# Attention scores of two heads at once in 64-row tiles, with the heads packed by pair, in an attention and MoE kernel on one core

## The chip, the core and the metric

The kernel runs on one core of one Trainium2 chip. The metric is the device time of one execution in microseconds (us), as the median of several runs. The profile is one further execution, taken by the hardware profiler.

## What is computed

Attention over 2 batches of 8 heads, with queries averaged by twos, then a dense mixture of four experts, then an ELU network. All is float32. Cut to what matters here:

```python
def _attn_ref(q, k, v):                      # (2, 8, 1152, 64) each
    q_pool = q.reshape(B, H, S // 2, 2, D).mean(axis=3)
    scores = np.matmul(q_pool, k.transpose(0, 1, 3, 2)) / np.sqrt(D)
    scores = scores - np.max(scores, axis=-1, keepdims=True)
    attn = np.exp(scores)
    attn = attn / (np.sum(attn, axis=-1, keepdims=True) + 1e-09)
    return np.matmul(attn, v)
...
x = attn_out.transpose(0, 2, 1, 3).reshape(B * S // 2, H * D)   # (1152, 512)
x = _moe_ref(x=x, domain_probs, w1, w2)      # sum over e of p_e * relu(x @ w1[e]) @ w2[e]
return _moe2_ref(x=x, w_in, w_out)           # ELU(x @ w_in) @ w_out
```

A head has 576 pooled queries, 1152 keys and a head dimension of 64.

## The kernel before, in words

The program has two stages. The first is the attention of 16 heads, two heads to a pair. The second, some two thirds of the time, is the MoE and the ELU network (called the MoE here): long runs of matmuls of 288 and 384 columns (line 1092) by a variant of Strassen's method, for which each quarter of the activations is split into a high and a low part and the two are multiplied crosswise.

Precise products are made in the same way in the attention. Queries and keys are split into a high part (rounded to the fast matmul type f32r) and a low part (the remainder). In `scores` (line 820) the contraction has 128 rows: `ks` holds the high part of a head's keys in rows 0 to 63 and the low part in rows 64 to 127, and `qs` holds the queries' high part in both halves, and then the low part in both halves. Two matmuls then give all four products of one head. The 1152 queries of a pair are cut into nine blocks of 128 rows (`m` from 0 to 8); block 4 holds the last 64 rows of one head and the first 64 of the other and takes four matmuls in place of two. A block's 1152 keys are taken in a part of 512 columns (`z` = 0) and one of twice 320 (`z` = 1), each with two PSUM buffers of its own.

Each block then runs through these steps, named by the letter that the planner uses:

- R (`max_all`, VectorE) takes the row maxima, E (`exp`, ScalarE, line 837) writes the exponentials to one of five tiles `e`.
- T (`transposes`, line 882) transposes 128x128 pieces, three to a PSUM bank `t`, of which there are two; D and G (`evac`, line 608 in a helper) copy them to the tile `pt` of the whole head, on ScalarE or VectorE.
- V (`values`, line 905) multiplies with the values when a whole head is transposed. An output has 64 rows (the head dimension), so two query halves of 288 columns go to the two halves of the array's columns: a form of the array of 128 rows by 64 columns. These are plain f32, and the program's one matmul is two instructions in the trace. O copies the result to `xo`.
- I, U, J, K, M, N form the softmax factors of a head. The step 3 writes them to DRAM (`dr`), the step 4 loads them back spread over the partitions (`fb`), X (`x_scaled`) multiplies, and the step m copies the head by DMA to its place in `acc`, the activations. The last two heads' X runs on VectorE.
- q, k, A, B, C, r, F, W, s load a pair's queries and keys, split them, and copy the two parts by DMA to the halves of `qs` and `ks`.

The order of all this on each engine is not written by hand: `order_of` plays the steps through with the costs in `STAGES` and ranks with the offsets in `MORE`, and the instructions are emitted in that order. The MoE has a planner of its own (`ffn_order`). Near the end of the attention, steps h and i already split two of the four quarters of `acc` for the MoE: x12 and x22 (quarters 8 and 3). x11 (heads 8 to 11 of the 16) and x21 (heads 12 to 15) are split in the MoE. Its first eight units use x12 and x22, the next four x11, and four more x21, whose parts go to a tile named `K`. Four PSUM banks `p` hold the running sums; each comes free when the hidden values in it were scaled (line 1151), rounded to `hh` and subtracted to `hl`.

Of the kernel before, what the change touches and what calls it, by code (L numbers as in the profile page):

```python
# [14 lines left out]
ALU = mybir.AluOpType  # L15
# [12 lines left out]
    "S": (dict(PE=465), 8),  # L28
    "R": (dict(DVE=690), 8),
    "E": (dict(ACT=790), 4),  # L30
    "I": (dict(DVE=220), 1.2),
    "U": (dict(POOL=400), 1.2),
    "J": (dict(ACT=250), 1.5),
    "K": (dict(POOL=600), 1.2),
    "M": (dict(DVE=200), 1.2),
    "N": (dict(POOL=400), 1.2),
    "3": (dict(SP=500), 2),
    "4": (dict(SP=1700), 2),
    "X": (dict(POOL=2300), 6),
    "T": (dict(PE=327), 2),  # L40
    "D": (dict(ACT=480, DVE=557), -3),
    "G": (dict(ACT=480, DVE=557), -4),
    "V": (dict(PE=2140), 6),
    "O": (dict(ACT=400, DVE=460), 0),
    "H": (dict(ACT=440), 8),
    "L": (dict(POOL=810), 3),
# [5 lines left out]
    "q": (dict(SP=450), -9),  # L52
    "k": (dict(SP=450), -9),
    "A": (dict(POOL=1430), -4),
    "B": (dict(ACT=690), -4),
    "C": (dict(DVE=800), -3),
    "r": (dict(SP=2400), -3),
    "F": (dict(ACT=690, DVE=470), -4),
    "W": (dict(POOL=1430), -3),
    "s": (dict(SP=2800), -3),  # L60
    "m": (dict(SP=2300), 8),
# [3 lines left out]
    "y": (dict(SP=600), 20),  # L65
# [3 lines left out]
    "i": (dict(POOL=2700, DVE=1250), 30),  # L69
# [4 lines left out]
AFTER = 240000  # L74

LAG = {"PE": 190, "ACT": 210, "DVE": 220, "POOL": 210, "SP": 9500}
LATE = {"3": 12000, "4": 11500, "r": 8000, "s": 8000, "X": 1200, "U": 900, "K": 700}

MIXED = {"D": dict(ACT=320, DVE=330), "G": dict(ACT=320, DVE=330)}
SECOND = {"S": dict(PE=585), "R": dict(DVE=822), "E": dict(ACT=920), "V": dict(PE=2620)}  # L80

LAST = {"X": dict(DVE=1100)}
MB = 9
NP = 5
CUT = 4

FIRST = [(x, i, z) for i in (0, 1) for x, z in (("q", 0), ("k", 0), ("k", 1), ("q", 1))]
FIRST = {x: 3800 + 1000 * n for n, x in enumerate(FIRST)}

BANKS = {"S0": 2, "S1": 2, "T": 2}  # L90
VBANK = "S0", "S0"

MORE = {
# [20 lines left out]
def blocks_of(i):  # L114

    return range(MB * (i // 2) + 4 * (i % 2), MB * (i // 2) + 5 + 4 * (i % 2))


def names_of(x, *k):

    k = list(k)
    p, m = divmod(k.pop(0), MB) if x in "SRETDG" and k else (0, 0)
# [3 lines left out]
    elif x in "qkABCrFWs":  # L126
        p, m, k = k[0], 0, k[1:]
# [5 lines left out]
def attention_ops(NH, KC):  # L133
# [87 lines left out]
    return ops  # L221


def order_of(ops):

# [1032 lines left out]
```

## Time and profile before

| | |
|---|---|
| median of 3 runs | 835.06 us (834.77 to 839.13) |
| profiled execution | 835.81 us, span 834.0 us |
| TensorE busy | 819.6 us, 98% of the span |
| VectorE, ScalarE, GpSimd busy | 589.3, 428.1, 322.4 us |
| attention, by the trace | first scores at 6.14 us, first matmul of the MoE at 248.25 us |

The span reaches from the first to the last instruction; what is left to the execution's own time lies around it. A matmul's duration in the trace reaches from its start to its modelled end, and successive matmuls overlap, so what one adds to a run of them is read from the distance of their starts or from a run's length, not from its duration.

### The profile page before, as it was taken

The numbers are of one execution on the slowest core, as the hardware profiler recorded it, in microseconds if no ns is written. First come the engines' busy times: TensorE is split into PE (matmuls) and PEld (weight loads), VectorE is DVE, ScalarE is ACT, GpSimd is POOL, SyncE is SP. The second block draws the span as 40 slices with busy tenths as digits, with TensorE's granted clock in tenths as the row PEclk, the third lists the DMA queues.
The fourth block names the chain that finished last, engine by engine and source line by source line (L and its number), as shares of the span: only waits on it lengthen the run. The fifth ranks groups of instructions, "written<-read, shape, count | busy, mean of one in ns | idle before, by whom it ended". The sixth has DMA issues, their size and how long they took to land.

```text
span 834.0 us, 14379 instructions
## 1 busy us (share of the span) xinstructions
PE 819.6 (98%) x5518; PEld 762.5 (91%) x5518; DVE 589.3 (71%) x922; ACT 428.1 (51%) x883; POOL 322.4 (39%) x344
## 2 busy tenths in 40 slices
PE   8999999999997999999999999999999999999998
PEld 7778777777767999999999999999999999999998
DVE  8777777767655849577685848577689857877472
ACT  6787677777763345141424324142434927455370
POOL 4353434344235726363644536263631231313000
PEclk9999999999999999999999999999999999999999
DMA  7999877864215224241422224241431324121002
GB/s 262 184 211 167 198 175 187 186 159 95 65 26 180 89 75 158 69 157 39 153 85 99 86 77 139 75 170 39 140 122 58 111 71 145 39 89 64 1 19 96
DMA packets 48356, 95.02 MB, mean 114 GB/s; under 512 B 14368, under 2 KB 26144, under 8 KB 45344
## 3 DMA queue, kind: packets, MB, share of 16 engines
q1 hardware_dynamic: 48000, 92.47, 39.8%
q10 hardware_dynamic: 288, 1.64, 0.7%
q8 instruction: 43, 0.70, 0.4%
q14 instruction: 25, 0.20, 0.1%
HBM read 64.37 MB, written 10.84 MB: 90 GB/s over the span
## 4 chain that ended last, share of the span: by engine, by line
PE 92%; DVE 3%; DMA 2%; ACT 2%; issue 0%; POOL 0%; SPq 0%; DVEq 0%
PE p L1092 66%; PE s L820 9%; PE s L905 8%; PE t L882 8%; DMA fb<-dr 1%; ACT e L837 1%; DMA q<-in 1%; ACT pt L608 1%; DVE hl L611 0%; DMA dr<-st 0%; DVE p L1151 0%; DVE st L831 0%; DVE K L611 0%; POOL st L611 0%; DVE acc L611 0%
## 5 line engine op out<-in xcount | busy, mean ns | idle before, releaser
L1092 PE MATMUL p<-hl,w2h 128*128 128x384 f32 x576 | 192.6, 334 | 0.5 <-DVE hl L611 0.5
L1092 PE MATMUL p<-hh,w2l 128*128 128x384 f32 x576 | 192.5, 334 | 0.0
L1092 PE MATMUL p<-hh,w2h 128*128 128x384 f32 x576 | 192.4, 334 | 0.0
L611 DVE TENSOR_TENSOR acc<-p,acc 128x768 f32<-128x768 f32 (+1 forms) x61 | 57.5, 942 | 89.5 <-PE p L1092 89.4
L831 DVE TENSOR_REDUCE st<-s 128x1 f32<-128x512 f32 (+1 forms) x144 | 105.4, 751 | 17.5 <-PE s L820 13.9
L1063 POOL TENSOR_TENSOR nt<-nt,ne 128x512 f32<-128x512 f32 x32 | 42.7, 1336 | 193.0 <-DVE ne L1059 193.0
L820 PE MATMUL s<-K,Q 128*128 128x320 f32 (+1 forms) x480 | 109.2, 355 | 0.7 <-ACT e L837 0.7
L837 ACT ACTIVATE e<-s,st 128x512 f32<-128x512 f32 (+1 forms) x144 | 106.5, 747 | 6.2 <-DVE st L831 3.3
L1092 PEld LDWEIGHTS p<-hl,w2h 128*128 128x128 f32 x576 | 108.1, 188 | 0.9 <-DVE hl L611 0.9
L1092 PEld LDWEIGHTS p<-hh,w2l 128*128 128x128 f32 x576 | 108.1, 188 | 0.0
L1092 PEld LDWEIGHTS p<-hh,w2h 128*128 128x128 f32 x576 | 108.1, 188 | 0.0
L882 PEld LDWEIGHTS t<-ident,e 128*128 128x128 f32 x648 | 75.3, 140 | 23.2 <-issue 7.4
L882 PE MATMUL t<-ident,e 128*128 128x128 f32 x648 | 93.7, 276 | 2.7 <-ACT e L837 2.0
L1092 PE MATMUL p<-K,wh 128*128 128x288 f32 x448 | 90.7, 296 | 0.0
L608 ACT CAST hh<-p 128x576 fp32r<-128x576 f32 x78 | 50.0, 641 | 69.8 <-DVE p L1151 66.9
L820 PEld LDWEIGHTS s<-K,Q 128*128 128x128 f32 x480 | 73.8, 189 | 7.3 <-issue 1.8
L905 PE MATMUL s<-pt,v 128*64 128x288 f32 x576 | 76.7, 411 | 0.0
L608 ACT COPY pt<-t 128x384 f32<-128x384 f32 (+1 forms) x126 | 55.3, 456 | 36.3 <-PE t L882 31.9
L1092 PEld LDWEIGHTS p<-K,wh 128*128 128x128 f32 x448 | 72.3, 189 | 0.3 <-DVE p L611 0.2
L1092 PE MATMUL p<-XH,wh 128*128 128x288 f32 x224 | 66.8, 298 | 5.6 <-DVE hl L611 5.1
L608 DVE COPY pt<-t 128x384 f32<-128x384 f32 (+1 forms) x114 | 56.0, 503 | 20.7 <-PE t L882 17.8
L1092 PE MATMUL p<-XH,wl 128*128 128x288 f32 x224 | 66.4, 296 | 0.0
(108 smaller groups left out, 1657.6 us busy)
## 6 DMA issues: line engine op xcount, KB each, us to landing
d<-in_va SPq DMA_DIRECT2D x16, 512.0 KB, 4.0
w<-nt SPq DMA_DIRECT2D x32, 256.0 KB, 3.4
d<-in_vb SPq DMA_DIRECT2D x16, 512.0 KB, 4.1
w<-w SPq DMA_DIRECT2D x8, 1024.0 KB, 4.8
Q<-q SPq DMA_DIRECT2D x28, 288.0 KB, 7.0
w<-in_wa SPq DMA_DIRECT2D x7, 1024.0 KB, 7.0
w<-in_wb SPq DMA_DIRECT2D x7, 1024.0 KB, 4.8
v<-in_v SPq DMA_DIRECT2D x16, 288.0 KB, 6.8
```

The costliest lines, as they stand in the source:

```text
L608: (nc.scalar.copy if e == "ACT" else engines[e].tensor_copy)(out, a)
L611: engines[e].tensor_tensor(out=out, in0=a, in1=b, op=op)
L820: nc.tensor.matmul(out=t[:, j], lhsT=q[:, o : o + P], rhs=ks[p % 2][:, y, c : c + PARTS[z][1]], start=k == x == 0, stop=2 * k + x == last,)
L831: nc.vector.tensor_reduce(out=nm[b, z], in_=s_t[b, z], axis=AX.XY, op=ALU.max, negate=True)
L837: nc.scalar.activation(et[b % NP][:, part(z)].rearrange("p (j k) -> p j k", j=PARTS[z][0]), s_t.pop((b, z)), AF.Exp, bias=nm.pop((b, z)), ...
L882: nc.tensor.transpose(t[:, c * P : c * P + P], et[b % NP][:, (3 * u + c) * P : (3 * u + c + 1) * P], ident)
L905: nc.tensor.matmul(out=tb[i, h][64 * z : 64 * z + 64, :HQ], lhsT=raws[i, "v"][:, c, :], rhs=pt[i % 2][:, c, half(z)], start=c == cs[0], st ...
L1063: nc.gpsimd.tensor_tensor(out=nt, in0=nt, in1=ne, op=ALU.add)
L1092: nc.tensor.matmul(out=out, lhsT=w[a][:, c, m * P : m * P + P], rhs=x[b][:, c], start=new and c == a + b == 0, stop=c == cs - 1 and a == 1 ...
```

## The change

It concerns the attention alone, and the splits that hand over to the MoE.

- The unit of work is no longer a block of one head but 128 queries of both heads of a pair (four units), and a tail unit with the last 64 queries of both. Rows 0 to 63 of `qs` and `ks` hold the pair's first head, rows 64 to 127 its second.
- `scores` makes three products of 64 rows for each head (high by high, high by low, low by high; low by low is dropped), the two heads in turn, into different PSUM banks: a form of the array of 64 rows by 128 columns, two tiles. In the tail unit, the queries of each head stand in their own rows and in 64 of the 128 columns, with zeros elsewhere, and three products of 128 rows do for both. A score step takes both PSUM buffers of its `z`.
- The parts are computed in place, by one operation for the two heads; the copies of queries and keys by DMA (r, s) are gone.
- Transposes stand four to a bank, and a fifth bank holds the last piece of both heads. Six tiles `e`, five tiles `pt` of one unit each.
- `values` works by unit: 128 columns (64 in the tail unit), the two heads in the two halves of the array's columns.
- The factors, their DMAs and X work by pair; X writes to `acc` itself, and the copy m is gone.
- x11 (quarter 1) is split in the attention too; the tiles of quarters 6 and 7 change place.
- Costs, ranks and a table of engines (`ON`) set a new order.

```diff
-        def scores(e, b, z, n):
-            p, m = divmod(b, MB)
-            s_t[b, z] = t = s_bank[z][n][:, :, : PARTS[z][1]]
-
-            hs = [0] * (m <= MH) + [1] * (m >= MH)
-            last = 2 * len(hs) - 1
-            q = qs[p % 2].rearrange("p y x q -> p (y x q)")
...
+        def scores(e, p, u, z, slots):
+            ts = [s_bank[z][n][:, :, : PARTS[z][1]] for _, n in slots]
+            rs = [slice(D * y, D * y + D) for y in (0, 1)] if u < QU else [slice(0, P)]
             for j in range(PARTS[z][0]):
                 c = part(z).start + j * PARTS[z][1]
-                for k, y in enumerate(hs):
-                    for x in (0, 1):
-                        o = P * m - Q * y + QW * (2 * y + x)
+                for a, b in ((0, 0), (0, 1), (1, 0)):
+                    for y, r in enumerate(rs):
+                        s_t[p, u, z, y] = ts[y]
                         nc.tensor.matmul(
-                            out=t[:, j],
-                            lhsT=q[:, o : o + P],
-                            rhs=ks[p % 2][:, y, c : c + PARTS[z][1]],
-                            start=k == x == 0,
-                            stop=2 * k + x == last,
+                            out=ts[y][:, j],
+                            lhsT=qs[p % 2][r, a, P * u : P * u + P],
+                            rhs=ks[p % 2][r, b, c : c + PARTS[z][1]],
+                            start=a + b == 0,
+                            stop=a == 1,
                         )
...
+        def transposes(e, p, u, t, slots):
+            tb[p, u, t] = b = bank[slots[0][1]]
+            blocks = [(t % 2, 4 * (t // 2) + c) for c in range(4)] if t < 4 else [(y, 8) for y in range(2 if u < QU else 1)]
+            for n, (y, c) in enumerate(blocks):
+                nc.tensor.transpose(b[:, n * P : n * P + P], ring(p, u, y)[:, c * P : c * P + P], ident)
...
             cs = range(CUT, KC) if h else range(CUT)
+            n = P if u < QU else TAIL
             for c in cs:
-                for z in (0, 1):
+                for y in (0, 1):
+                    x = unit(p, u)[:, c]
                     nc.tensor.matmul(
-                        out=tb[i, h][64 * z : 64 * z + 64, :HQ],
-                        lhsT=raws[i, "v"][:, c, :],
-                        rhs=pt[i % 2][:, c, half(z)],
+                        out=tb[p, u][head(y), h * P : h * P + n],
+                        lhsT=raws[p, y][:, c, :],
+                        rhs=x[:, y] if u < QU else x[:, 0, y * TAIL : y * TAIL + TAIL],
                         start=c == cs[0],
                         stop=c == cs[-1],
                     )
...
+        def x_scaled(e, p):
+            x = xo[p % 2]
+            tt(e, x, x, fb[p % 2].rearrange("p q z -> p z q"), ALU.mult)
+            tt(e, acc[:, p % PB, p // PB * Q : p // PB * Q + Q], x[:, 0], x[:, 1], ALU.add)
...
-    for n, (x, need) in enumerate([(8, early), (3, early + old)]):
-        op(w + n, need, "h", x, after=AFTER)
+    for n, (x, ps) in enumerate([(8, (0, 1)), (3, (2, 3)), (1, (4, 5))]):
+        need = [("X", p) for p in ps] + [("S", NPR - 2, u, z) for u in range(5) for z in (0, 1)] * (x == 3)
+        op(w + n, need, "h", x, after=AFTER)
         op(w + n, [("h", x)], "i", x)
...
-                if g or i in (1, 2):
+                if g or i == 2:
...
-    "S": (dict(PE=465), 8),
+    "S": (dict(PE=700), 8),
...
+ON = {
+    "a0": "DVE", "d0a": "ACT", "a1": "DVE", "a1a": "DVE", "d1a": "ACT", "e1": "POOL", "e1a":
...
```

The order on TensorE in the middle of the attention, before (`s` scores, `t` transposes; where `pt` and `v` are read, value products, two of them side by side; the size is that of the output):

```order
L882 MATMUL t_118<-ident,e_110 128x128 x3
L882 MATMUL t_117<-ident,e_112 128x128 x3
L905 MATMUL s_119<-pt_115,v 64x288 x10
L882 MATMUL t_118<-ident,e_112 128x128 x3
L882 MATMUL t_117<-ident,e_113 128x128 x3
L820 MATMUL s_120<-K_76,Q_124 128x512 x2
L820 MATMUL s_119<-K_76,Q_124 128x512 x2
```

The same engine and a like place, near the end of the attention, after the change (of a score step only the first two of its matmuls, one for each head):

```order
L914 MATMUL t_119<-ident,e_113 128x128 x4
L934 MATMUL t_120<-pt_114,v 64x128 x10
L859 MATMUL s_122<-K_73,Q_75 128x512
L859 MATMUL s_121<-K_73,Q_75 128x512
...
L914 MATMUL t_119<-ident,e_110 128x128 x4
L914 MATMUL t_120<-ident,e_108 128x128 x4
L859 MATMUL s_123<-K_73,Q_75 128x320
L859 MATMUL s_124<-K_73,Q_75 128x320
```

Scores and transposes, which both used the whole array, now use it in two forms, and value products come more often and are shorter. Over the whole program the form changes 61 times before (31 times into the values' form, 30 times out of it), and 250 times after (73 into the values' form, 72 out of it, 105 between the 64-row form and the whole array).

The order on VectorE at the end of the attention, before (`xo` and `fb`: the last heads' scaling; `p` with `pb`: the scaling of hidden values; `hl`: their low part, which frees a bank; `K`, `XL`: splits of quarters; `ne`, `nt`: preparation of later weights):

```order
L611 TENSOR_TENSOR xo_133<-xo_133,fb_137 128x576
L611 TENSOR_TENSOR xo_133<-xo_133 128x288
L611 TENSOR_TENSOR acc<-acc 128x2x288
L1151 SCALAR_TENSOR_TENSOR p_2684<-p_2684,pb 128x2x288
L1151 SCALAR_TENSOR_TENSOR p_2685<-p_2685,pb 128x2x288
L611 TENSOR_TENSOR hl<-p_2684,hh 128x2x288
L611 TENSOR_TENSOR hl<-p_2685,hh 128x2x288
L1151 SCALAR_TENSOR_TENSOR p_2686<-p_2686,pb 128x2x288
L611 TENSOR_TENSOR K_76<-acc,K_76 128x2x288 x2
L611 TENSOR_TENSOR hl<-p_2686,hh 128x2x288
```

And after:

```order
L694 TENSOR_TENSOR xo_134<-xo_134,fb_136 128x1152
L694 TENSOR_TENSOR acc<-xo_134 128x576
L1160 SCALAR_TENSOR_TENSOR p_3035<-p_3035,pb 128x2x288
L1160 SCALAR_TENSOR_TENSOR p_3036<-p_3036,pb 128x2x288
L1160 SCALAR_TENSOR_TENSOR p_3037<-p_3037,pb 128x2x288
L694 TENSOR_TENSOR hl<-p_3035,hh 128x2x288
L694 TENSOR_TENSOR hl<-p_3036,hh 128x2x288
L1048 TENSOR_SCALAR ne<-d 128x512
L694 TENSOR_TENSOR hl<-p_3037,hh 128x2x288
L1160 SCALAR_TENSOR_TENSOR p_3038<-p_3038,pb 128x2x288
```

The scaling of the last pair is one product and one sum of twice the size, and the splits into `K` have moved to GpSimd.

## Rows read from the trace of the kernel before

**Rows 1.** The page: busy us (share of the span) xinstructions.

```profile
PE 819.6 (98%) x5518; PEld 762.5 (91%) x5518; DVE 589.3 (71%) x922; ACT 428.1 (51%) x883; POOL 322.4 (39%) x344
```

**Rows 2.** Busy time by stretch: engines' us (instructions), granted clock, DMA share, GB/s.

```profile
24.00:240.00 216.00, 214.52 (x1549) 165.49 (x1549) 158.56 (x299) 162.55 (x421) 83.55 (x155) 1.00 0.71 154
...
sum 240.00, PE 236.30 PEld 181.54 DVE 178.27 ACT 181.04 POOL 95.25; mean PE 78.77 PEld 60.51 DVE 59.42 ACT 60.35 POOL 31.75
```

**Rows 3.** Groups of instructions: form, count, busy us, mean ns of one.

```profile
L882 PE MATMUL t<-ident,e 128*128 128x128 f32 x648 | 93.7, 276 | 2.7 <-ACT e L837 2.0 <-ACT pt L608 0.8
...
L905 PE MATMUL s<-pt,v 128*64 128x288 f32 x576 | 76.7, 411 | 0.0
...
L820 PE MATMUL s<-K,Q 128*128 128x320 f32 x320 | 62.1, 323 | 0.7 <-ACT e L837 0.7
...
L820 PE MATMUL s<-K,Q 128*128 128x512 f32 x160 | 51.0, 420 | 0.0
```

**Rows 4.** The chain that ended last, 56 to 65 us: start, length, piece.

```profile
56.72 2.09 PE s L905 x16
58.81 0.81 PE t L882 x6
59.62 2.58 PE s L905 x20
...
63.00 0.93 PE s L820 x4
63.93 0.66 PE t L882 x6
```

**Rows 5.** The same chain, 124 to 136 us.

```profile
125.14 2.58 PE s L905 x20
127.72 0.67 PE s L820 x2
...
133.70 1.17 PE s L820 x8
```

**Rows 6.** Groups of instructions: the evacuations of 384 columns.

```profile
L608 ACT COPY pt<-t 128x384 f32<-128x384 f32 x106 | 49.5, 482 | 33.0 <-PE t L882 30.9 <-DVE st L831 0.8
...
L608 DVE COPY pt<-t 128x384 f32<-128x384 f32 x86 | 47.1, 553 | 14.4 <-PE t L882 13.1
```

**Rows 7.** TensorE in order of time: first scores, then the first MoE units.

```profile
6.14 1.17 PE L820 MATMUL s<-K,Q 128*128 128x512 f32 x4
...
248.25 0.40 PE L1092 MATMUL p<-XH,wh 128*128 128x288 f32 x1 [0.50 <-ACT xo L608]
...
263.18 0.40 PE L1092 MATMUL p<-XH,wh 128*128 128x288 f32 x1 [1.95 <-DVE hl L611]
...
267.79 0.40 PE L1092 MATMUL p<-XH,wh 128*128 128x288 f32 x1 [1.17 <-DVE hl L611]
...
271.59 0.40 PE L1092 MATMUL p<-XH,wh 128*128 128x288 f32 x1 [1.96 <-DVE hl L611]
```

**Rows 8.** VectorE in order of time, 258 to 272 us.

```profile
258.54 0.76 DVE L611 TENSOR_TENSOR xo<-xo,fb 128x576 f32<-128x576 f32 x1 [11.34 <-DMA fb<-dr]
...
259.71 0.75 DVE L611 TENSOR_TENSOR acc<-acc 128x576 f32<-128x576 f32 x1
...
262.37 1.41 DVE L611 TENSOR_TENSOR hl<-p,hh 128x576 fp32r<-128x576 f32 x2
...
264.37 2.70 DVE L611 TENSOR_TENSOR K<-acc,K 128x576 fp32r<-128x576 f32 x2
...
270.79 0.74 DVE L611 TENSOR_TENSOR hl<-p,hh 128x576 fp32r<-128x576 f32 x1
```

**Rows 9.** Busy time by stretch, 272 to 276 us.

```profile
272.00:276.00 4.00, 4.00 (x20) 4.00 (x20) 2.36 (x3) 0.62 (x1) 1.42 (x2) 0.57 0.39 98
```

**Rows 10.** DMA issues: count, KB each, median us to landing.

```profile
Q<-q SPq DMA_DIRECT2D x28, 288.0 KB, 7.0
...
fb<-dr SPq DMA_DIRECT2D x32, 144.0 KB, 6.2
```

More of the change, by code (lines that the diff above doesn't have):

```diff
@@ L208, in attention_ops @@
+    for p in range(NPR):
+        b = MB * p + 8
+        op(b, [("E", *x[:2], z, x[2]) for x in rows if x[0] == p for z in (0, 1)], "I", p)
+        for x, y in zip("UJKMN", "IUJKM"):
+            op(b, [(y, p)], x, p)
+        op(b, [("N", p)], "3", p)
+        op(b, [("3", p), p > 1 and ("X", p - 2)], "4", p)
+        op(b, [("O", p, u) for u in range(5)] + [("4", p)], "X", p)
     op(0, [], "l", after=40000)
     op(0, [("l",)], "p")
-    w = NB - 30
+    w = MB * NPR - 30
     for j in range(8):
-        op(w + j, [("S", w + j, 0)], "w", j)
+        op(w + j, [("S", NPR - 4, 0, 0)], "w", j)
@@ L265, in order_of @@
         for o, t in ready.items():
-            x = takes(o)
-            if x:
-                if not banks[x]:
+            pools, n = takes(o)
+            if n:
+                waits = [sorted(banks[x].values())[n - 1] for x in pools if len(banks[x]) >= n]
+                if not waits:
                     continue
-                t = max(t, min(banks[x].values()))
-            _, e = min((max(t, free[e]) + n, e) for e, n in of(o).items())
+                t = max(t, min(waits))
+            _, e = min((max(t, free[e]) + n, e) for e, n in costs[o].items())
             best.append((max(t, free[e]), ops[o][1], place[o], o, e))
@@ L274, in order_of @@
         del ready[o]
-        free[e] = start + of(o)[e]
-        end[o] = free[e] + (SOON if e == "SP" and o[1:] >= (12,) else LATE.get(o[0], LAG[e]))
-        x, bank = takes(o), None
-        if x:
-            bank = min(banks[x], key=lambda n: (banks[x][n], n))
-            del banks[x][bank]
-            holds[o] = x, bank
+        free[e] = start + costs[o][e]
+        end[o] = free[e] + end_of(o, e)
+        pools, n = takes(o)
+        slots = []
+        if n:
+            x = min((x for x in pools if len(banks[x]) >= n), key=lambda x: sorted(banks[x].values())[n - 1])
+        for y in range(n):
+            slot = min(banks[x], key=lambda n: (banks[x][n], n))
+            del banks[x][slot]
+            holds[o, y] = x, slot
+            slots.append((x, slot))
         back = gives(o)
         if back:
-            x, n = holds.pop(back[0])
-            banks[x][n] = back[1]
-        out.append((start, len(out), o, e, bank))
+            x, n = holds.pop(back)
+            banks[x][n] = end[o]
+        out.append((start, len(out), o, e, slots))
         for y in after[o]:
@@ L591, in attention_then_moe_then_elu_ffn @@
     ks = [const.tile([P, 2, 2 * HN], F32R, name="K%d" % j) for j in range(2)]
+    qs = [const.tile([P, 2, HN + 64], F32R, name="Q%d" % j) for j in range(2)]
     x12, x22, x11, x21 = (acc[:, 2 * c : 2 * c + 2, HN * n : HN * n + HN] for n in (0, 1) for c in (0, 1))
@@ new lines, in load_k, with load_v @@
+        def load_k(p, z=None):
+            k = raw_k
+            for y in (0, 1):
+                src = kT[p // PB, p % PB]
+                if z is None:
+                    nc.sync.dma_start(
+                        out=k[head(y)].rearrange("d (z k) -> d z k", z=2),
+                        in_=src[:, y].rearrange("(z d) k -> d z k", z=2),
+                    )
+                else:
+                    nc.sync.dma_start(out=k[head(y), z * KQ : z * KQ + KQ], in_=src[head(z)][:, y])
+        def load_v(e, p, y):
+            raws[p, y] = t = v_p.tile([P, KC, D], F32, tag="v%d" % y, name="v")
+            nc.sync.dma_start(out=t, in_=v[p // PB, 2 * (p % PB) + y])
@@ L699, in attention_then_moe_then_elu_ffn @@
+        et = [e_p.tile([P, KC * P], F32, name="e%d" % j) for j in range(NE)]
+        pt = [e_p.tile([P, KC, 2, P], F32, name="pt%d" % j) for j in range(NT)]
         bank = [ps_t.tile([P, 512], F32, name="t%d" % j) for j in range(2)]
```

545 lines of the change are left out of this document (233 added, 312 removed), and 102 rows, old and new, of tables (MORE, ON).

## The prediction

> **What bounds the kernel now.** I read the page's first part, then the busy time by stretch, then the chain that ended last, then the waits where the chain leaves TensorE. TensorE is busy for 98% of the span [rows 1], which alone says little, so the attention is looked at by itself: it runs from the first scores at 6.14 us to the first matmul of the MoE at 248.25 [rows 7]. In 24 to 240 us TensorE has work in 214.52 of 216 us, VectorE in 158.56 and ScalarE in 162.55 [rows 2]; from 8 to 248 us TensorE is without work for 240 - 236.30 = 3.7 us [rows 2]. So the attention is bound by TensorE, the other two engines have about a quarter of their time to spare, and whatever TensorE is given or spared there moves the end.
>
> What one step costs it is read from the chain, where pieces follow each other without gaps. Six transposes take 0.66 us, 0.109 each; four scores of 512 columns 0.93, 0.2325 each [rows 4]; eight of 320 columns 1.17, 0.146 each [rows 5]. Value products come in pieces of 16 and 20 instructions, 2.09 and 2.58 us [rows 4]: the difference gives 0.1225 each, and 16 x 0.1225 = 1.96 leaves 0.13 us that belongs to the start of the piece. Their 288 columns at a transpose's pace (0.109 for 128, both plain f32) would take 0.245. They step at half of that because they are 64 columns wide in the array and two run side by side. That is the evidence here that the array can be shared. The price of sharing is beside it: the six transposes behind a value piece take 0.81, not 0.66, so 0.15 us goes when the array leaves the halved form, and 0.13 when it enters. Two scores behind a value piece take 0.67 [rows 5] where 0.465 is their due: 0.20.
>
> Check: 160 x 0.2325 + 320 x 0.146 = 83.9 for scores, 576 x 0.1225 = 70.6 for values, 648 x 0.109 = 70.6 for transposes (counts in [rows 3]), 31 entries and 30 leavings of the halved form (counted in the whole order) 8.5: 233.6 us, with 3.7 of idle time 237.3, and 241.6 us lie between the first scores and the last value product (0.50 before 248.25 [rows 7]). The prices hold to 2%.
>
> **The change, part by part.** *Scores.* Before, a product had 128 rows: high and low part of K stacked, two products (q high, q low) for a head. Now a head has 64 rows and three products, and the two heads of a pair take the two halves of the rows. If the halves run side by side as the columns' halves do, a pair of matmuls costs one step. Steps of 512 columns: 32 units x 3 + 8 tails x 3 = 120; of 320: 240. 120 x 0.2325 + 240 x 0.146 = 62.9, that is 21.0 us less than 83.9.
>
> *Values and transposes.* 648 transposes stay. The values become 576 products of 128 columns and 144 of 64, two instructions each as now (288 products, 576 instructions, [rows 3]). By columns, 1152 x 0.0544 + 288 x 0.0272 = 70.5: nothing gained or lost. The bound on the other side: if the 64-column instructions step no faster than the 128-column ones, 288 x 0.0272 = 7.8 us more. I take the lower end, since everything measured here goes by columns from 128 to 512. The Trainium skill (TensorEngine Tiling (Array Packing), Instruction Overhead) gives a floor of about 60 cycles a matmul, which 64 columns just clear; by it, too, the addition would be near zero.
>
> *Changes of form.* This is the term against the change. The order has 61 changes before. Now the array alternates between 64-row scores, whole transposes and 64-column values: 250 changes, 73 into the values' form, 72 out of it, and 105 between the 64-row form and the whole array. The first 145 have their prices: 73 x 0.13 + 72 x 0.15 = 20.3. The 105 are not in this trace. Bounds: nothing (the array need not empty between row forms) and 0.20 each (the dearest change shown, the one onto a score [rows 5]), so 0 to 21 us. I take 0.15, the nearest row, because what shows at a column change is that the first weight load of the new form starts only after the last product has run out, and I see no reason for which a change by rows would be different: 15.8. Together 36.1 against 8.5: 27.6 us more. The Trainium skill (the same page, Tiling Modes, Key Properties) says that changing the mode, not just the tile, drains TensorE. For the columns this trace agrees, with 0.13 to 0.20 us; for rows no run here shows it. By the rule the sum is the one that I make; without it, 15.8 us less.
>
> *Engines beside.* The evacuations go from 240 of mostly 384 columns to 184 of mostly 512, for as many columns; 482 and 553 ns for 384 [rows 6] is then an upper bound by column, and both engines have a quarter free. A score step now takes both banks of its half and so waits for both exponentials of the unit before; transposes, values and the other half's scores are put in between. I leave the 3.7 us of idle time, give or take 3. The copies that doubled q and k by DMA (28 of 288 KB for q alone, 7.0 us to land [rows 10]) and those of the outputs go; they lie beside a busy TensorE, so I cost them at nothing. If that cover were gone, one late pair would cost some 7 us once.
>
> *The hand-over to the MoE.* Eight first units of the MoE run from 248.25 to about 261. Then TensorE waits three times for `hl`, 1.95 + 1.17 + 1.96 us, and starts again at 271.59 [rows 7], at a granted clock of 0.57 over 4 us (part of them at 1.2 GHz) [rows 9], 4 x 0.43 = 1.7 us more: 6.8 us in all. The cause is VectorE: the last head's scaling waits for its factors until 258.54, 10.8 us after the last value product, and behind it are queued the scaling's sum, the MoE's evacuations and the split of x21 into `K`, 2.70 us [rows 8]; the fourth bank comes free at 271.5, 23.8 us after the attention. Now x11 is split during the attention, GpSimd takes the splits into `K`, and VectorE holds only the scaling (both heads: twice 0.76 and 0.75 for the sum, 2.2), three first evacuations, then `hl`. With factors at +10.8, the first bank is free at 10.8 + 2.2 + 4 x 0.7 = +15.8 (+15.4 now), the fourth, behind three more `hl`, an evacuation and two steps of the weights' narrowing (`ne`, `nt`), six at about 0.7, near +20: 4 us earlier. Bounds: the factors of two heads come in one transfer of twice the bytes (6.2 us a piece now [rows 10]), 3 us later at worst, so a gain of 1; or, with the slow clock gone too, 5.5. I take 4.
>
> **Sum.** -21.0 + 0 + 27.6 - 4 = +2.6 us. The profiled execution took 835.81 us (span 834.0), so 838.4; it lies 0.75 above the median of the three runs, 835.06, so about **837.6 us**. The MoE and the last stage, 66% of the chain, are the same instructions.
>
> **The rivals.**
> *A, changes between row forms cost nothing.* For it: they are not in the trace, and the values' form also halves the width of the output, which row tiles don't. Against it: entry and exit both cost, whatever stands behind. 15.8 less: 822 us.
> *B, the rows' halves don't run side by side.* Then 216 x 0.2325 + 432 x 0.146 = 113.3 instead of 62.9: 50.4 more, 888 us. Against it: the columns' halves do.
> *C, slower: the narrow value products don't go by columns.* Place: the tail unit of each pair, 18 products of 64 columns. Price 7.8, 845 us; it decides from a step of 0.033 us an instruction on (0.0272 by columns), where 288 x 0.006 = 1.7 us more carry the 837.6 over 0.5%.
>
> **How the numbers follow.** The likeliest is the sum, within 0.5% (about what a measurement of this kernel can tell from no change, 4.2 us): chance 0.47, its own range 833 to 843 from idle time and hand-over; of it 0.07 falls below and 0.08 above the 0.5%. A: 0.30. C: 0.15. B: 0.05. The rest, 0.03, I count as slower. Faster 0.07 + 0.30 = 0.37, same 0.32, slower 0.08 + 0.15 + 0.05 + 0.03 = 0.31. The range reaches from A with the larger hand-over gain (818) to C with the smaller (848); B stays outside.
>
> **What would show it.** Two scores of one pair start within a few ns of each other, and a 512-column piece of six takes about 0.70 us plus a change. The first transpose behind a 64-row score shows the 0.15 us, or doesn't (A). TensorE's idle time in the attention stays about 4 us. The first MoE matmul comes 2 to 11 us later than 248.25; if it comes earlier, A holds. The three waits for `hl` shrink to about two. Wrong would be a TensorE that waits in mid-attention for exponentials: then the pairs, not the array, bound it.

## The result and the profile after

| | before | changed |
|---|---|---|
| median, in one series | 835.35 us (834.77 to 839.13, 5 runs) | **844.53 us** (843.35 to 846.37, 5 runs) |
| profiled execution, its span | 835.81, 834.0 us | 846.37, 844.6 us |
| first scores | 6.14 us | 6.74 us |
| first matmul of the MoE | 248.25 us | 258.88 us |
| from there to the end of the span | 585.75 us | 585.72 us |

The ratio is 1.0102 with an interval of 1.0075 to 1.0128: the changed kernel is 1% slower. The forecast was 837.6 us, 818 to 848. So the time lies inside the range, but 7 us above the forecast and just above the 833 to 843 that the text gave to its likeliest case. The profiled execution was the slowest of the five, so the two profiled spans lie 10.6 us apart where the medians lie 9.2.

The last two rows of the table place the loss. From the first scores to the first matmul of the MoE the attention took 258.88 - 6.74 = 252.1 us, against 242.1 before: 10.0 more, where the forecast had -21.0 + 27.6 = 6.6 more. Behind it nothing was gained, where the forecast had 4 us. The scores start 0.6 us later.

TensorE still bounds the attention. The page's first part and the busy time by stretch (engines PE, PEld, DVE, ACT, POOL; granted clock, DMA share, GB/s) answer to [rows 1] and [rows 2]:

```profile
PE 830.9 (98%) x6550; PEld 776.3 (92%) x6550; DVE 584.2 (69%) x883; ACT 415.3 (49%) x827; POOL 328.4 (39%) x283
```

```profile
8.00:10.00 2.00, 0.94 (x8) 0.79 (x8) 2.00 (x3) 1.20 (x3) 1.16 (x1) 0.71 0.95 286
10.00:12.00 2.00, 2.00 (x14) 1.67 (x11) 1.20 (x3) 0.85 (x4) 0.00 (x0) 0.50 1.07 370
24.00:240.00 216.00, 214.58 (x2366) 169.07 (x2364) 159.18 (x264) 145.62 (x356) 96.64 (x100) 1.00 0.33 75
260.00:270.00 10.00, 10.00 (x78) 10.00 (x77) 2.12 (x2) 2.22 (x4) 1.46 (x2) 1.00 0.40 92
270.00:280.00 10.00, 5.79 (x30) 5.57 (x30) 6.54 (x9) 5.24 (x11) 7.27 (x6) 0.75 0.76 290
```

TensorE in order of time shows what a change of form costs. The columns are the start, the length up to the last matmul's modelled end, and the piece; what a piece takes of TensorE is read from start to start:

```profile
84.80 1.09 PE L914 MATMUL t<-ident,e 128*128 128x128 f32 x8
85.82 0.96 PE L859 MATMUL s<-K,Q 64*128 64x512 f32 x6
86.72 0.66 PE L914 MATMUL t<-ident,e 128*128 128x128 f32 x4
87.30 1.14 PE L859 MATMUL s<-K,Q 64*128 64x320 f32 x12
88.37 1.09 PE L934 MATMUL t<-pt,v 128*64 128x128 f32 x16
89.40 0.44 PE L914 MATMUL t<-ident,e 128*128 128x128 f32 x2
89.77 1.31 PE L934 MATMUL t<-pt,v 128*64 128x128 f32 x20
91.01 0.66 PE L914 MATMUL t<-ident,e 128*128 128x128 f32 x4
```

Six scores of 64 rows and 512 columns and the four transposes behind them take from 85.82 to 87.30, 1.48 us. Side by side, the scores are three steps of 0.2325, and the transposes four of 0.109: 1.13. So the halves of the rows do run in pairs (six steps alone would be 1.40), and two changes cost 0.35. From 88.37 to 91.01 lie 36 value instructions and two transposes, by the columns 36 x 0.0544 + 0.22 = 2.18: 2.64 - 2.18 = 0.46 for three changes. Worked out in this way from all starts between 20 and 220 us of the attention, a piece of 64-row scores between transposes takes 0.201 us more than its steps (median of 33 pieces), a piece of transposes behind such scores 0.150 (20 pieces), one of value products between transposes 0.155 (38) and one of transposes behind those 0.150 (26).

Behind the attention stand these rows of TensorE, VectorE and ScalarE's queue, which answer to [rows 7] and [rows 8]:

```profile
258.88 0.40 PE L1101 MATMUL p<-XH,wh 128*128 128x288 f32 x1 [0.47 <-ACT xo L691]
...
276.06 0.61 PE L1101 MATMUL p<-XH,wh 128*128 128x288 f32 x1 [4.21 <-DVE hl L694]
```

```profile
265.14 1.36 DVE L694 TENSOR_TENSOR xo<-xo,fb 128x1152 f32<-128x1152 f32 x1 [8.91 <-DMA fb<-dr]
266.53 0.76 DVE L694 TENSOR_TENSOR acc<-xo 128x576 f32<-128x576 f32 x1
273.26 2.10 DVE L1160 SCALAR_TENSOR_TENSOR p<-p,pb 128x576 f32<-128x576 f32 x3 [5.97 <-DMA pb<-pr]
```

```profile
267.37 0.37 ACTq L1095 DMA_DIRECT2D pb<-pr  x1
267.78 0.67 ACT L691 CAST x7h<-acc 128x576 fp32r<-128x576 f32 x1 [8.96 <-DVE acc L694]
```

And this one of ScalarE's queue in the kernel before:

```profile
248.03 0.35 ACTq L1086 DMA_DIRECT2D pb<-pr  x1
```

The last pair's scaling ends at 267.3, 8.4 us behind the first MoE matmul. Before, the last head's ended at 259.71 + 0.75 = 260.5 [rows 8], 12.2 us behind it. But the first evacuation of the MoE does not follow it: it waits another 5.97 us for the probabilities (`pb`), whose load was issued only at 267.37. Before, it was issued at 248.03, 0.2 us ahead of the first MoE matmul. In the program `pb` lies in a pool that takes room which the attention's pools give back. By the sizes of the tiles, the attention's pool with `xo` and `fb` has grown from under 12 KB to 28 KB a partition and now reaches under the pool that holds `pb`, so that the load has to wait for the last scaling; that this is the reason is read from the program, and no run changes the sizes alone. TensorE has one wait in place of three, 4.21 us instead of 1.95 + 1.17 + 1.96 = 5.08 [rows 7], and behind this wait a clock of 0.75 in 270 to 280, after 1.00 in 260 to 270 (a mean of its two levels, 1.2 and 2.4 GHz).

### The profile page after: what moved, and what is told of

Read it like the earlier page. It is cut to its first block, busy times and chain, and to the rows that moved or that the text cites. A ratio compares the mean times of both kernels' runs of the same rounds, so it can differ in the third digit from the quotient of the medians.

```text
span 844.6 us, 16174 instructions
## 1 busy us (share of the span) xinstructions
PE 830.9 (98%) x6550; PEld 776.3 (92%) x6550; DVE 584.2 (69%) x883; ACT 415.3 (49%) x827; POOL 328.4 (39%) x283
## 4 chain that ended last, share of the span: by engine, by line
PE 95%; DMA 2%; DVE 1%; SPq 0%; issue 0%; ACT 0%; POOL 0%; DVEq 0%; ACTq 0%
PE p L1101 66%; PE t L914 10%; PE s L859 9%; PE s L934 5%; PE t L934 4%; DMA pb<-pr 1%; DMA dr<-st 1%; DMA fb<-dr 0%; DMA rk<-in_k 0%; DVE p L1160 0%; DVE hl L694 0%; DVE pt L691 0%; SPq L786 0%; DVE p L694 0%; POOL K L694 0%
## 5 line engine op out<-in xcount | busy, mean ns | idle before, releaser
L914 PE MATMUL t<-ident,e 128*128 128x128 f32 x648 | 99.2, 284 | 1.8 <-DVE pt L691 1.8
L914 PEld LDWEIGHTS t<-ident,e 128*128 128x128 f32 x648 | 70.3, 141 | 27.1 <-issue 15.4
L859 PE MATMUL s<-K,Q 64*128 64x320 f32 (+3 forms) x648 | 85.0, 360 | 1.8 <-POOL K L694 1.1
L691 ACT COPY pt<-t 128x512 f32<-128x512 f32 (+2 forms) x97 | 51.6, 535 | 67.5 <-PE t L914 67.1
L859 PEld LDWEIGHTS s<-K,Q 64*128 64x128 f32 (+1 forms) x648 | 55.4, 187 | 15.2 <-issue 10.8
L1101 PE MATMUL p<-XL,wh 128*128 128x288 f32 x224 | 67.1, 299 | 0.0
L694 POOL TENSOR_TENSOR wl<-w,wh 128x512 fp32r<-128x512 f32 x33 | 43.6, 1336 | 59.9 <-ACT wh L691 59.9
```

What stands on the lines that cost most here:

```text
L691: (nc.scalar.copy if e == "ACT" else engines[e].tensor_copy)(out, a)
L694: engines[e].tensor_tensor(out=out, in0=a, in1=b, op=op)
L859: nc.tensor.matmul(out=ts[y][:, j], lhsT=qs[p % 2][r, a, P * u : P * u + P], rhs=ks[p % 2][r, b, c : c + PARTS[z][1]], start=a + b == 0, s ...
L914: nc.tensor.transpose(b[:, n * P : n * P + P], ring(p, u, y)[:, c * P : c * P + P], ident)
L1101: nc.tensor.matmul(out=out, lhsT=w[a][:, c, m * P : m * P + P], rhs=x[b][:, c], start=new and c == a + b == 0, stop=c == cs - 1 and a == 1 ...
```

## The experiments

The theory after this result: the changes between the 64-row form and the whole array cost nearly 0.18 us each, not 0.15, and the hand-over gained nothing because a load took the place of the wait that went. Rivals: the price belongs to something else that came with the pairs (twice as many weight loads, scores and transposes taking turns); and the hand-over is bound elsewhere. Times of the runs are medians; the kernel before took 835.5 to 836.5 in their series. The code cuts are shortened, with `...` where something is left out.

**Whole scores.** One matmul over all 128 rows in the place of each pair.

```
-    for a, b in ((0, 0), (0, 1), (1, 0)):
-        for y, r in enumerate(rs):
-            matmul(out=ts[y][:, j], lhsT=qs[r, a, ...], rhs=ks[r, b, ...])
+    for n, (a, b) in enumerate(((0, 0), (0, 1), (1, 0))):
+        y = int(n > 0 and len(rs) == 2)
+        matmul(out=ts[y][:, j], lhsT=qs[:, a, ...], rhs=ks[:, b, ...])
```

> The changed kernel with one score matmul over all 128 rows in the place of each pair of 64-row ones; it leaves out the separation of the two heads, so their scores are sums over both. As many steps on TensorE, as many columns, the same order, the same work on the other engines; only the 105 changes between 64-row form and whole array are gone. Theory: such a change costs 0.20 us onto a score and 0.15 back, so 105 x 0.175 = 18 us less than the changed kernel, 826 (823 to 829), the first MoE matmul near 240.5 instead of 258.88, and the first transpose behind a score follows at its pace. Rival: the steps seen behind a 64-row score come from the exchange of weights or from scores and transposes taking turns, not from the form: then the time stays within 4 us of the changed kernel.

827.5 us (825.84 to 830.52, 4 runs). TensorE in order of time, with the start of the scores and of the MoE:

```profile
6.63 1.42 PE L859 MATMUL s<-K,Q 128*128 128x512 f32 x4 [1.01 <-ACT Q L812]
...
86.44 0.60 PE L914 MATMUL t<-ident,e 128*128 128x128 f32 x4
86.79 0.94 PE L859 MATMUL s<-K,Q 128*128 128x512 f32 x3
87.57 0.60 PE L914 MATMUL t<-ident,e 128*128 128x128 f32 x4
...
239.89 0.40 PE L1101 MATMUL p<-XH,wh 128*128 128x288 f32 x1 [0.47 <-ACT xo L691]
```

Four transposes and three steps of scores take from 86.44 to 87.57, 1.13 us, which is the bare sum: no price is left. The attention takes 239.89 - 6.63 = 233.3 us, 18.9 less: **0.18 us for each of the 105 changes** (0.17 against the run with the probabilities apart, whose attention took 251.5; by the medians of the whole kernel it is 17.0 us, 0.16 each). Over all pieces the scores take 0.088 more than their steps and the transposes 0.081 less (49 and 35 pieces), together nothing. Scores and transposes take turns here as before, so that is not the cause. But the scores have half as many weight loads here, so this run alone doesn't tell the loads from the form.

**Whole value products too.**

```
-    for y in (0, 1):
-        matmul(out=tb[head(y), ...], lhsT=raws[p, y][:, c, :], rhs=x[:, y])
+    matmul(out=tb[:, ...], lhsT=raws[p, c % 2][:, 2 chunks of 64], rhs=x[:, c % 2])
```

> As the run before, and the value products too go over the whole array: one product of 128 columns of V in the place of each pair of 64; it leaves out that each head is multiplied by its own V. No change of form is left in the attention. Theory: the 145 changes into and out of the values' form cost 0.145 us each, so 21 us less than with whole scores alone, some 805 us, if TensorE stays the bound; up to 8 us of that may go into waits for the exponentials and evacuations, since VectorE would then be busy some 75% of the attention. Rival: the value products' starts cost what they cost for another reason (a first weight load that nothing hides): then less than 6 us is gained over whole scores.

815.0 us (813.88 to 815.81, 4 runs): 12.5 less than with whole scores, the attention 227.71 - 6.69 = 221.0, 12.2 less. The theory wanted 21. What it had missed stands in two rows, the products of 64 columns in this run, and, second, in the changed kernel:

```profile
37.92 0.82 PE L914 MATMUL t<-ident,e 128*128 128x128 f32 x6
38.58 2.12 PE L933 MATMUL s<-pt,v 128*128 128x64 f32 x18
40.53 1.04 PE L914 MATMUL t<-ident,e 128*128 128x128 f32 x8
```

```profile
44.21 1.27 PE L934 MATMUL s<-pt,v 128*64 128x64 f32 x36
45.41 1.09 PE L914 MATMUL t<-ident,e 128*128 128x128 f32 x8
```

Over the whole array 18 products of 64 columns take 1.95 us, 0.108 each, as much as products of 128 columns; in halves 36 take 1.20, changes included, and by their steps (0.058 a pair, by the starts in the trace) 18 x 0.058 = 1.05. So 0.90 us is lost in each of the eight pairs, 7.2 us in all. What all pieces of the attention take beyond their steps falls from 25.0 us with whole scores to 4.9 here: 20.1 us for the 145 changes, 0.139 each, where the theory had 0.145. TensorE's idle time grows by 0.7; 20.1 - 7.2 - 0.7 = 12.2, as measured. The theory holds with that correction.

**Transposes in the scores' form.** The other way to take the 105 changes out, which leaves nothing out of the computation: each block as two transposes of 64 rows, one into each of two banks. In the trace 27 changes come in instead, between these transposes and the tails' whole scores, so that 172 are left of 250.

```
-    transpose(b[:, n * P : n * P + P], e[:, c * P : c * P + P], ident)
+    for x in (0, 1):
+        transpose(b[:, x, n * D : n * D + D], e[head(x), c * P : c * P + P], ident[head(x), head(x)])
```

> The changed kernel with its transposes in the form of its scores: each block of 128 x 128 as two transposes of 64 rows, side by side, the first into one bank, the second into the other; the order, the evacuations and everything else stay. The 105 changes between 64-row form and whole array become none, the 145 around the value products stay. Theory: it is the change of form that costs, so they take 105 x 0.18 = 19 us with them; and a pair of 64 columns steps between 0.055 us (by its columns, as the pairs of value products do) and 0.109 (a weight load of 128 columns, the 0.107 that whole products of 64 columns took with everything over the whole array), so the 648 blocks cost between 35 us less and nothing more: 790 to 826 us, and I take 0.109, so 825. Rival 1: what costs is that scores and transposes take turns, or their weights: then only the step counts, 809 to 845. Rival 2: the two weight loads of a pair don't run side by side, a step of 0.2: 60 us more, 885.

851.2 us (849.98 to 853.03, 4 runs): slower, by no case that was expected. Busy time in 24 to 240 us, TensorE's waits in the attention (us in total, times, longest), and pieces in order of time, with two of VectorE's copies:

```profile
24.00:240.00 216.00, 188.94 (x2916) 151.08 (x2913) 155.70 (x262) 143.81 (x352) 91.13 (x96) 0.99 0.32 73
```

```profile
PE t L916 <- DVE pt L691: 19.3, 34, 1.5
PE t L916 <- ACT pt L691: 6.3, 14, 0.7
PE t L939 <- DVE pt L691: 3.6, 8, 0.9
```

```profile
98.43 0.71 PE L916 MATMUL t<-ident,e 64*128 64x64 f32 x16 [0.43 <-DVE pt L691]
99.07 1.15 PE L860 MATMUL s<-K,Q 128*128 128x320 f32 x6
...
120.38 0.71 PE L916 MATMUL t<-ident,e 64*128 64x64 f32 x16
121.14 1.29 DVE L691 COPY pt<-t 128x512 f32<-128x512 f32 x2 [0.22 <-PE t L916]
...
122.57 0.47 PE L916 MATMUL t<-ident,e 64*128 64x64 f32 x8 [0.64 <-DVE pt L691]
```

TensorE is busy for 188.94 us instead of 214.58, less, as the theory says, and it waits 29 us for evacuations, which the changed kernel hardly did. The cause of the waits is the new layout: the two buffers are now halves of the same two banks, in one tile. At 120.38 both halves are filled; the next transposes, into the first half, start at 122.57, only when VectorE has emptied both (121.14 + 1.29). The copies themselves are as fast as before (687 ns on VectorE for 512 columns in either run). Whether the common tile or the common banks make them wait, no run tells. Eight pairs of transposes take 0.64 us, the change to the tail's whole scores included; by the starts in the trace a pair steps at 0.059, half of a whole block's 0.109. And a piece of transposes between two pieces of 64-row scores takes 0.02 us more than its steps (median of 22), where a whole one takes 0.150. The scores behind them still take 0.085 more where no wait stands behind them, instead of 0.201: so a turn from transposes to scores and back costs about 0.1 us, where the changed kernel pays 0.35. Twice as many weight loads are there, and most of the price is not: what costs is, for the most part, the change of form.

**The probabilities apart.** `pb` gets room of its own, and is loaded on SP's queue during the attention.

```
+    pb = const.tile([P, T], F32, name="pb")
...
+    if (x, *k) == ("w", 7):
+        nc.sync.dma_start(out=pb, in_=pr[0].unsqueeze(0).to_broadcast([P, T]))
```

> The changed kernel with one thing moved: the copy of the probabilities to all partitions (pb) has room of its own and is loaded during the attention, instead of in room that the attention gives back. Theory: at the hand-over to the MoE, VectorE's first evacuation stood behind this load (5.97 us without work until 273.26, TensorE's 4.21 until 276.06 behind that). With pb there, the first evacuation starts when the last scaling ends, near 267.3, the first hl is ready near 270.1, before the eight first units of the MoE end (271.85). So TensorE's wait of 4.21 falls below 1 us and its clock, 0.83 over the 20 us after 270, stays above 0.93: 4 to 7 us less than the changed kernel, 837.5 to 840.5. Rival: another wait takes its place (the weights in_wb, issued by ScalarE behind the load; GpSimd's low parts): then less than 1.5 us is gained, 843 or more.

843.2 us (840.87 to 843.9, 4 runs): 1.3 less, inside the rival's bound. VectorE, GpSimd and TensorE in order of time:

```profile
265.62 0.76 DVE L695 TENSOR_TENSOR acc<-xo 128x576 f32<-128x576 f32 x1
266.30 0.76 DVE L1162 SCALAR_TENSOR_TENSOR p<-p,pb 128x576 f32<-128x576 f32 x1
...
277.15 1.66 DVE L1064 TENSOR_TENSOR nt<-nt,ne 128x512 uint32<-128x512 uint32 x1
...
280.17 1.83 DVE L695 TENSOR_TENSOR acc<-acc 128x576 f32<-128x576 f32 x1
281.93 1.77 DVE L1070 SCALAR_TENSOR_TENSOR ne<-d,ne 128x512 f32<-128x512 uint32 x1
```

```profile
276.78 6.37 POOL L695 TENSOR_TENSOR w2l<-w,w2h 128x512 fp32r<-128x512 f32 x4
```

```profile
276.50 0.40 PE L1103 MATMUL p<-XH,wh 128*128 128x288 f32 x1 [0.49 <-DVE hl L695]
287.09 0.44 PE L1103 MATMUL p<-hh,w2h 128*128 128x384 f32 x1 [2.37 <-DVE hl L695]
```

The load was a wait: with it gone, the evacuation follows the scaling at once, and of the 4.21 us 0.49 are left. Another takes its place, as the rival said, though neither of the two that it named: 2.37 us behind VectorE's narrowing steps and sums, slow while GpSimd works. From the first MoE matmul to the end it is 841.7 - 258.01 = 583.7, 2.0 us less.

**The narrowing later.** The first piece of the narrowing is planned 10 us later.

```
-    at = 2000 + PACE * k
+    at = 2000 + PACE * k + 10000 * (k == 0)
```

> The kernel with the probabilities loaded early, and the first piece of the narrowing of the later weights planned 10 us later, so that on VectorE the first evacuations of the MoE stand ahead of it. With the probabilities early, TensorE still waits 0.49 and 2.37 us for hl, the second behind 8 us of narrowing steps and sums on VectorE (277 to 284 us, each two to three times its 0.42 to 0.75 us while GpSimd works). Theory: VectorE's queue is what bounds the hand-over, so the 2.37 goes and the clock stays at 1.00: 3 to 4 us less than with the probabilities alone, some 839.5. Rival: VectorE's sums and splits, which stay ahead, hold the second evacuations as long: less than 1 us.

853.7 us (852.11 to 855.43, 4 runs), 10 more than with the probabilities alone. The planner moved much besides: TensorE waits 1.40 and 3.44 us for `hl`, and again after 330 us, where the changed kernel doesn't. The run says nothing on the queue; it fails as an experiment.

**The start.**

```
-WARM = 11
+WARM = 13
...
+    if (x, *k) == ("e", 0, 1):
+        e = "DVE"
```

> The changed kernel with its start alone changed: the low part of the second half of k on VectorE instead of GpSimd (0.75 instead of 1.41 us), and 13 warming matmuls instead of 11. Theory: the wait of 1.06 us before 9.21 shrinks to some 0.4, the 0.76 us before 6.74 is filled with work, the granted clock no longer falls to 0.50 in 10 to 12 us, and the kernel takes 1 to 3 us less than the changed one, with the first MoE matmul near 257. Rival: the first units wait for exponentials whatever TensorE does, so the gap moves behind the scores: less than 0.5 us.

844.2 us (843.07 to 845.55, 4 runs), no difference: the rival. The wait before the second scores fell from 1.06 to 0.38 us, and two waits of 0.42 and 0.40 for exponentials came behind them. The clock of 0.71 and 0.50 at 8 to 12 us was 1.00 here, but so it was in the run with the probabilities apart, whose start is the changed kernel's. The run with transposes as pairs, which starts like the changed kernel, shows the slow clock again (0.80 and 0.50). So it belongs to single executions, the profiled one among them.

**Fewer changes.** The planner's step for TensorE now counts 0.165 us for a change of form, and the numbers that rank the steps were searched again (`PEN`, in ns; probabilities apart in this run and those below).

```
+    new = e == "PE" and form_of(o) != form
...
+    if e == "PE" and form_of(o) != form:
+        start += PEN - EARLY
```

> The kernel with the probabilities early, and its attention in a new order from the same planner, which now counts 0.165 us for each change of form and was searched again: 226 changes instead of 250; instructions and forms are those of the changed kernel. Theory: 24 changes fewer at 0.165 give 4 us, so 839 instead of 843.2 (836 to 842), if the waits in the attention stay at some 4 us. Rival: the waits that the old order avoided come back, which the plan shows only roughly: 843 or more.

837.6 us (836.06 to 841.73, 10 runs), 5.6 less; the profiled spans lie 841.7 - 834.3 = 7.4 apart. The attention gave 2.5 us of that (251.5 to 249.1), less than the theory's 4. The rest came from the hand-over, which I had not foreseen:

```profile
255.76 0.37 PE L1028 MATMUL p<-XH,wh 128*128 128x288 f32 x1 [0.62 <-DVE xo L617]
```

```profile
257.55 1.36 DVE L620 TENSOR_TENSOR xo<-xo,fb 128x1152 f32<-128x1152 f32 x1 [1.93 <-DMA fb<-dr]
258.94 0.76 DVE L620 TENSOR_TENSOR acc<-xo 128x576 f32<-128x576 f32 x1
```

The new order has the last pair's factors ready earlier: the scaling ends 3.9 us behind the first MoE matmul instead of 8.4, TensorE has no wait for `hl` at all up to 300 us, and from that matmul to the end it is 834.3 - 255.76 = 578.5 us, 7.2 less than in the changed kernel.

**Both together.** Transposes as pairs, in pieces for both heads, so that each bank is evacuated by one copy; an order planned for that.

```
-    blocks = [(t % 2, 4 * (t // 2) + c) for c in range(4)] if t < 4 else ...
+    blocks = [(y, c) for c in range(4 * t, min(4 * t + 4, KC)) for y in (0, 1)]
     for n, (y, c) in enumerate(blocks):
+        for x in (0, 1):
+            transpose(b[x][:, n * D : n * D + D], e[y][head(x), c * P : c * P + P], ident[head(x), head(x)])
```

> The transposes as pairs of 64 rows again (0.059 us a pair in the trace, 0.033 from a transpose to a score), now in pieces for both heads, so that each bank holds one half of the rows and is evacuated in one copy, and in an order planned for that: 113 to 117 changes of form instead of 250, of value products against the rest alone; probabilities early. TensorE's own work in the attention: 62.9 scores, 648 x 0.059 = 38 transposes, 72 values, 117 x 0.165 = 19 changes, 192 us instead of the 242 from first score to last product. Theory: TensorE then no longer bounds it alone; the two transposing banks are one buffer, and VectorE and ScalarE (159 and 146 us in 216 before) have to keep up. The plan ends as late as that of the run before within 2 us: so near 838, 828 to 848. Rival: TensorE waits for evacuations as with pairs in the old order (30 us in the attention): 850 or more.

841.4 us (840.95 to 844.47, 4 runs): inside the theory's range and not the rival's. TensorE waits 15.4 us for evacuations (up to 300 us), half of what it did in the old order, its clock over 24 to 240 us is 0.96, and the last scaling ends 11.7 us behind the first MoE matmul.

> As the run before, in an order planned with half the delay from one engine to the next (0.11 us behind VectorE and ScalarE instead of 0.21): 138 changes of form. Theory as for the run before; if real delays are nearer to these, its waits are shorter and it is faster than the run before by up to 10 us, 828 to 840; if not, it is slower than it.

835.4 us (833.76 to 838.92, 10 runs), 6 less than the run before, as the theory had it for shorter delays, and level with the kernel before (ratio 0.9999, 0.998 to 1.0018). Its attention is the shortest of the kernels that compute the whole, 245.47 - 7.04 = 238.4 us, but its scaling ends 11.5 us behind the first MoE matmul and the MoE takes 587.0. So the search got the end of the last scaling as a second aim.

> Transposes as pairs of 64 rows as in the two runs before, in an order searched with one more aim: that the last pair's scaling ends soon after the last value product (by the plan 2.8 us behind it; in the run before 9.3, in the run with fewer changes 3.0). In the traces the MoE took 578.6 us from its first matmul to the end where the scaling was planned 3.0 us behind, 583.7 to 587.0 where it was 8 to 9 behind. Theory: the hand-over is bound by when the last scaling ends, so the MoE takes 579 to 581 here, the attention 240 (planned 1.7 us longer than the run before's 238.4): 7 minus 2 us less than the run before, some 829 (826 to 832). Rival: the hand-over waits for VectorE's narrowing steps and GpSimd's low parts in any case: 835 or more.

**828.4 us** (826.81 to 829.77, 6 runs), as expected; ratio to the kernel before 0.9909, interval 0.9888 to 0.9929: it beats both kernels. Rows of TensorE, the end of the last scaling on VectorE, TensorE's largest wait (5 to 300 us), and busy time:

```profile
7.03 1.27 PE L790 MATMUL s<-K,Q 64*128 64x512 f32 x8 [1.42 <-ACT Q L743]
...
80.61 0.71 PE L846 MATMUL t<-ident,e 64*128 64x64 f32 x16
81.14 0.98 PE L790 MATMUL s<-K,Q 64*128 64x512 f32 x6
...
246.31 0.40 PE L1032 MATMUL p<-XH,wh 128*128 128x288 f32 x1 [0.39 <-DVE xo L622]
```

```profile
249.09 0.76 DVE L625 TENSOR_TENSOR acc<-xo 128x576 f32<-128x576 f32 x1
```

```profile
PE s L790 <- ACT e L803: 5.7, 11, 2.5
```

```profile
24.00:230.00 206.00, 197.02 (x3012) 164.62 (x3010) 158.93 (x296) 152.89 (x390) 97.03 (x104) 0.98 0.40 82
```

Eight pairs of transposes take 81.14 - 80.61 = 0.53 us, where the steps of eight whole blocks alone take 0.87. The attention takes 239.3 us and the MoE 825.0 - 246.31 = 578.7. Against the run with fewer changes, whose MoE takes as long, the attention is 9.8 us shorter: that is what the paired transposes and their order give. TensorE now has 9 us without work in 206, mostly for exponentials: it no longer bounds the stage alone.

> As the run before it in this call, planned with 0.07 us from VectorE and ScalarE to the next engine instead of 0.11: planned scaling 2.7 us behind the last product, 140 changes of form instead of 133. Theory and rival as there: 826 to 833, and which of the two is faster tells which delay is nearer to the chip's.

828.4 us (825.78 to 832.85, 6 runs): the same, so which delay is nearer to the chip's stays open.

## Why the prediction came out as it did

*What bounds the kernel*: right. TensorE is busy for 214.58 of 216 us, and all that moved in the attention moved by its steps and changes.

*Scores, -21.0*: right. In the trace the two scores of a pair start 3 ns apart (median), and three pairs and four transposes take 0.35 us above the 1.13 that whole scores take in their place, which is the price of two changes. Rival B is out.

*Values, 0*: right. The 64-column products go nearly by columns in halves, 0.029 us an instruction where the sum had 0.0272 and rival C 0.0544: 0.6 us in all. Its mechanism exists, but over the whole array: 0.108 us a product there.

*Changes of form, +27.6*: the mechanism right, one price too low. The changes between the rows' form and the whole array cost 0.201 onto the scores and 0.150 back, 0.17 to 0.18 in the mean, not 0.15 (0.16 by the medians), so 105 of them 17 to 19 us instead of 15.8. The bound of 0.20 held, rival A is out. I had the row for it: 0.20 onto a score [rows 5] was the price of half the changes, and I took the one onto a transpose for all. The Trainium skill (TensorEngine Tiling (Array Packing), Tiling Modes, Key Properties) says that a change of mode drains the engine. The runs here agree, for rows with 0.16 to 0.18 us, and find 0.02 us to pay from scores to transposes of the same form and 0.085 back.

*Idle time and start*: idle time as foreseen; the start not looked at. The scores begin 0.6 us later, and the profiled execution lost another 0.6 us (252.1 against 251.5) with a slow clock near 10 us, which the execution of the run with the probabilities apart doesn't show.

*The hand-over, -4*: this step failed, and it is half of the error. It put the factors at +10.8 us behind the last value product and counted VectorE's queue from there. They landed earlier than that (the scaling began at 265.14, 6.7 us behind the last value product). But the sum gave the load of the probabilities no term: it took it as done, as it was before, when it was issued 0.2 us ahead of the first MoE matmul. Now it stood behind the scaling, and VectorE waited 5.97 us for it; by the tiles' sizes, because packing the heads by pair had enlarged the pool that the scaling works in. Net gain 0. That the load is a wait is shown by the run that moves it; that the next wait is VectorE's is seen in that run's rows. That the end of the last scaling sets what the hand-over costs is borne out by six orders with the probabilities apart:

| run | scaling ends behind the first MoE matmul | the MoE takes |
|---|---|---|
| both together, end of the scaling as second aim, 0.07 us | 2.5 us | 578.7 us |
| the same, 0.11 us | 3.5 us | 578.7 us |
| fewer changes | 3.9 us | 578.5 us |
| probabilities apart | 8.4 us | 583.7 us |
| both together, half the delay | 11.5 us | 587.0 us |
| both together, the first order | 11.7 us | 587.3 us |

Up to about 4 us the MoE takes no longer, and beyond it about 1 us more for each. These orders differ in other things too, but the first two of the table were searched for an early end of the scaling, and their time was forecast from it. It is not all: with the narrowing moved, the scaling ends at 8.8 us and the MoE takes 593.5.

The account of the profiled spans: 6.6 foreseen in the attention, about 2.6 for the dearer changes, 0.6 for the clock, 0.6 for the later start, 0 for the hand-over: 10.4 of 844.6 - 834.0 = 10.6.

The chances stood near to even between faster, same and slower. The likeliest case, within 0.5% of the kernel before, missed by another half a per cent, and both of its errors had the same sign. That the range held all the same is in part luck: its upper end came from rival C, which did not happen, and left room for an error that no rival named. Its lower end is 2 us wider than its terms give (837.6 - 15.8 - 1.5 = 820).

## What to carry to other kernels

Sharing TensorE's array by rows or columns doubles what a step does, and each change of form took 0.13 to 0.20 us back here, so count the changes in the order of instructions before counting the steps saved, and look for neighbours that can take the same form: here transposes of 64 rows in pairs paid twice. When tiles grow or pools are packed anew, go through each load that follows the stage and ask whose room it now takes. A wait at a hand-over between stages is worth chasing to the chain that ends it (the last factors) rather than to the instruction that shows it.

## What the runs showed of the hardware

Two transposes of 64 rows and 64 columns, side by side, step at 0.059 us, a whole block at 0.109. A product of 64 columns over the whole array takes 0.108 us, as long as one of 128 columns, while two of them side by side in halves step at 0.058. VectorE's `ne<-d,ne` and `acc<-acc` took 1.77 and 1.83 us while GpSimd worked on `w2l`, 0.68 and 0.75 at a free moment (277 us in the order with fewer changes). In the changed kernel's trace all seven `acc<-acc` with nothing on GpSimd beside them took 0.75 us, and three of four with work beside them 1.85. And TensorE's clock was 0.71 in 8 to 10 us and 0.50 in 10 to 12 (1.2 GHz throughout) in the profiled execution of the changed kernel, and 1.00 (2.4 GHz) in that of the run with the probabilities apart, which has the same start and the same wait of 1.07 us ahead of 9.21.
